# Raw float64 weight blocks converted in pairs: one VectorE shift, one mask and one ScalarE reading over 1024 elements instead of two over 512

## The chip, the cores and the metric

One core of a Trainium2 chip runs the whole program: TensorE (PE, matmuls; its weight loads are PEld), VectorE (DVE), ScalarE (ACT), GpSimd (POOL) and SyncE (SP), which issues most of the DMAs. The metric is the device time of one launch in microseconds. The kernel before took 1313.93 to 1318.08 us in three runs, median 1317.09 us.

## What is computed

```python
# 1 attention, 4 batches x 8 heads x 576 tokens x 64, of each row the 32 largest scores
scores = scale * q @ k.T; keep = scores >= kth_largest(scores, 32)
x = softmax(where(keep, scores, -1e9)) @ v          # -> 2304 tokens x 512
# 2 gated layer; w_a, w_b [512, 1536] and w_out [1536, 512] arrive as float64
x = ((x @ w_a) * (x @ w_b)) @ w_out
# 3 one of 8 experts per token, chosen by cosine with expert_emb; gate = its softmax weight
out[t] = gate[t] * (relu(x[t] @ w1[e]) @ w2[e])
```

[...] A block of 128x512 weights is loaded as raw 64-bit words and its bits are put together to float32 by integer work; the float32 number is then split into two float32r parts (high and low), and each product of the gated layer is the sum of three matmuls over these parts.

## The kernel before, in words

**Attention runs in steps.** One step treats one tile of 128 attention rows; there are 144. For a tile TensorE makes scores, ScalarE copies them to `s`, VectorE takes the 32 largest (`topk`, lines 369 to 391: four MAX8 and three MATCH_REPLACE8 over 576 elements), ScalarE and GpSimd make the softmax weights (`softmax`, lines 393 to 403), TensorE turns and multiplies them. In step n VectorE does the first half of tile n and the second half of tile n-1, woven together.

**The weights are converted beside the first 30 steps or so.** `Blocks` (line 492) holds 36 blocks in a fixed order: (0,f) and (1,f) are column blocks of w_a and w_b, (2,f) row blocks of w_out. A block goes through: loading of the raw words by SP (line 515, 512 KB); a ScalarE reading of the low words (line 535); on VectorE a shift with a mask of the high words (line 538) and a second mask (line 539); a GpSimd addition that gives float32 in `x1T` (line 543); a ScalarE rounding to the high part (line 551); two TensorE passes (lines 554 and 555) and a ScalarE copy for the low part (line 556); for w_a and w_b a store to DRAM (line 558), from which later token groups read them again. The code has one state per block (`at`): `open` issues line 535, `start` lines 538, 539 and the next load, and each call of `stage` moves a block on by one: to 2 (addition), 3 (line 551), 4 (lines 554 to 558).

**Buffers.** Two raw blocks (`raw64`, RB = 2), two of each half-product (`w64t`, `w64r`, TB = 2), two of `x1T` (XB = 2), four of `wab` (WB = 4). A raw buffer is free when lines 535, 538 and 539 of its block have read it; only then SP can issue the load that takes its place. `may` also holds a w_a or w_b block back until the gated layer of the first token group has come to hidden block f-1 (`begun`).

**Order.** TensorE, VectorE, ScalarE and GpSimd execute in the order in which the Python code emits; SP's queue is ordered by a planner with priorities. In a step the code emits VectorE's `topk`, then five slots of TensorE work with `background` work of the gated layer between them; `conv.stage()` is called in slots 0, 2 and 4, `conv.open()` in slot 3, and `conv.start()` at the step's end. From step 16 on two blocks are started per step, before that one in every second step. A second use of `raw64`: token groups with odd number take two of these buffers for their input (line 618), and so does the first expert (line 1157).

After attention the remaining token groups and then the experts run, almost on TensorE alone.

Of the kernel before, what the change touches and what calls it, by code (L numbers as in the profile page):

```python
# [26 lines left out]
GN = 256  # L27
# [16 lines left out]
RB = 2  # L44
FOLD = (0,)
PEN = (0,)
PC = 512
TB = 2
UEV = 2.6
EARLY = 6  # L50
# [24 lines left out]
FG = 100000  # L75
# [7 lines left out]
def fused_kernel(  # L83
# [18 lines left out]
    pe, dve, act, pool, sp = nc.tensor, nc.vector, nc.scalar, nc.gpsimd, nc.sync  # L102
# [93 lines left out]
    mk = mo.enter_context(tc.tile_pool(name="mk", bufs=2))  # L196
    mp = mo.enter_context(tc.tile_pool(name="mp", bufs=2, space=PSUM))

    with ExitStack() as ph:
        wk = ph.enter_context(tc.tile_pool(name="wk", bufs=2, side="right"))  # L200
# [291 lines left out]
        class Blocks:  # L492
# [3 lines left out]
            def __init__(self):  # L496
                self.order = [(i, f) for f in range(2) for i in range(2)] + [(2, f) for f in range(EARLY)]
                for f in range(2, NF):
                    self.order += [(0, f), (1, f)] + [(2, f + EARLY - 2)] * (f + EARLY - 2 < NF)
                self.raw, self.tiles, self.begun, self.at, self.going = [], {}, 0, [], []  # L500

            def fetch(self, n):
                while len(self.raw) < min(n, len(self.order)):
                    i, f = self.order[len(self.raw)]
                    if i < 2:
                        src = (w_a, w_b)[i][:, f * P : (f + 1) * P].rearrange("(c p) j -> p c j", p=P)
                    else:
                        src = w_out[f * P : (f + 1) * P, :].rearrange("p (c j) -> p c j", c=KC)
                    if src.dtype == F32:
                        raw = mk.tile([P, KC, P], F32, name="raw64", bufs=RB)  # L510
                        sp.dma_start(raw, src)
                    else:
                        raw = mk.tile([P, KC, P, 2], I32, name="raw64", bufs=RB)
                        with tc.high_priority(offset=2 * FG if len(self.raw) < EL else FG):
                            sp.dma_start(raw.rearrange("p a n t -> p a (n t)"), src.bitcast(I32))
                    self.raw.append(raw)

            def may(self, k):

# [6 lines left out]

            def block(self, k):
                i, f = self.order[k]
                raw = self.raw[k]
                if raw.dtype == F32:  # L530
                    x = raw
                else:
                    lo, hi = raw[:, :, :, 0], raw[:, :, :, 1]
                    r = wk.tile([P, KC, P, 2], I16, name="w64r", bufs=TB)
                    act.activation(r[:, :, :, 0], lo.bitcast(U32), AF.Copy, scale=2.0**-29)
                    yield
                    t = wk.tile([P, KC, P], I32, name="w64t", bufs=TB)
                    dve.tensor_scalar(t, hi, 3, 0x3FFFFFFF, op0=OP.logical_shift_left, op1=OP.bitwise_and)
                    dve.tensor_scalar(r[:, :, :, 1], raw.bitcast(I16)[:, :, :, 3], -0x4000, None, op0=OP.bitwise_and)
                    self.fetch(k + 1 + RB)  # L540
                    yield
                    x = mk.tile([P, KC, P], F32, name="x1T", bufs=XB)
                    pool.tensor_tensor(x.bitcast(I32), t, r.rearrange("p a n t -> p a (n t)").bitcast(I32), op=OP.add)
# [12 lines left out]
                act.activation(lo, p.rearrange("p (c j) -> p c j", c=KC), AF.Copy)  # L556
                if i < 2:
                    sp.dma_start(wab_d[i, f], wt.bitcast(F32).rearrange("p a c j -> p (a c j)"))

# [3 lines left out]
                    self.stage()  # L563

            def ready(self, *block):
                return block in self.order[: sum(a == 4 for a in self.at)]

            def open(self):

                k = len(self.at)  # L570
                if k < len(self.order) and sum(a < 2 for a in self.at) < TB:
                    self.fetch(k + RB)
                    self.going.append(self.block(k))
                    self.at.append(0)
                    if self.raw[k].dtype != F32:
                        next(self.going[k])
# [10 lines left out]
            def stage(self):  # L587

                for k in range(len(self.at)):
                    if 0 < self.at[k] < 4 and self.may(k):  # L590
                        next(self.going[k], None)
                        self.at[k] += 1

        conv = Blocks()
# [6 lines left out]
        class Group:  # L601
# [5 lines left out]
            def inputs(self):  # L607
                if self.xg:
                    return
                g0, N = GROUPS[self.gi]  # L610
                self.xg = []
                if self.gi == 0 and DIRECT:
                    self.xg = xg0
                    return
                conv.need(1, NF - 1)
                for i, d in enumerate((xh_d, xl_d)):
# [295 lines left out]
        for step in range(-AHEAD_L, NRW + TL + 5):  # L912
            now[0] = step
            if step + AHEAD_L < NRW:
                b, pr, part, first, last, kind, c, slot = rows[step + AHEAD_L]
# [6 lines left out]
            if 0 <= step + AHEAD_P < NRW:  # L922
                b, pr, part, first, last, kind, c, slot = rows[step + AHEAD_P]
# [9 lines left out]
            j = step - 2  # L933
# [3 lines left out]
            with tc.high_priority(offset=FG):  # L937
                next(soft, None)
                soft = softmax(live[step - 2]) if 0 <= step - 2 < NRW else none
                j = step - 5  # L940
                if 0 <= j < NRW and rows[j][4] and made[rows[j][:3]].n >= F0 * NP:
                    sums(made[rows[j][:3]], False)
                j = step - 3
# [12 lines left out]
                elif 0 <= step < NRW:  # L956
                    thresholds[0] = cur
            if step == -AHEAD_L:
                conv.fetch(RB)
# [16 lines left out]
            if i != turned[0] + 1:  # L976
                i = -1
# [15 lines left out]
            for slot_, g in enumerate((tg, sg, tg, mg, sg)):  # L993
                if g is not none and not run(g) and g is mg and mixes:
                    mixes.pop(0)
                    mg = none
                with tc.high_priority(offset=FG):
                    if slot_ == 1 or slot_ == (2 if mg is not none else 3):
                        next(soft, None)
                    if slot_ in (0, 2, 4) and step >= 2:  # L1000
                        conv.stage()
                    if slot_ == 3:
                        for _ in range(pace):
                            conv.open()
                if slot_ in (2, 4):
                    piece()
# [21 lines left out]
            for _ in range(pace):  # L1028
                with tc.high_priority(offset=FG):
                    conv.start()  # L1030
            while done < len(GROUPS) and (sum(GROUPS[done]) <= ready[0] or (done == 0 and ready[0])):
                w = step + (D0 if done == 0 else RD)
                todo.append([w, Group(done, w), None])
                if done and len(todo) < 3 and conv.ready(1, NF - 1):
                    todo[-1][1].inputs()
                    if len(todo) == 1:
                        todo[-1][1].load()
                done += 1
        order.__exit__(None, None, None)

    with ExitStack() as ph:
# [111 lines left out]
        def first_expert():  # L1153

            ids = wx.tile([P, 2, 2], I32, name="ids0")
            sp.dma_start(ids, idv[0, : 2 * P, :].rearrange("(t p) c -> p t c", p=P))
            xs = [mk.tile([P, PC // KC * KC * 2], F32, name="raw64", bufs=RB)[:, :RW] for _ in range(2)]
# [103 lines left out]
        for e in range(1, NE):  # L1261
            nx = gather(e + 1) if e + 1 < NE else None
            xs, xT = x
# [97 lines left out]
```

## Time and profile before

| | us |
|---|---|
| median of three runs | 1317.09 |
| profiled execution | 1316.72 |
| its span, first to last instruction | 1315.0 |
| PE busy | 1173.2 |
| DVE busy | 921.4 |
| ACT busy | 820.2 |
| POOL busy | 720.9 |
| mean granted TensorE clock | 0.965 of full |

The busy times are averages over stages with different limits, so the table alone does not say what sets the end. The profile splits the span into windows and shows there which engine has no idle time left; it also shows, per instruction, what ended the idle time before it.

### The profile page before, as it was taken

Reading aid. Unit: us, or ns where it says so; the run is one execution under the profiler, and the core shown is the slowest. Engines: PE = TensorE matmul, PEld = TensorE weight load, DVE = VectorE, ACT = ScalarE, POOL = GpSimd, SP = SyncE. Lnnn points to the kernel's source line nnn. Section 1 sums busy time; section 2 is a strip of 40 time slices with the busy share of each in tenths; the row PEclk is TensorE's granted clock in tenths of the full one; section 3 lists DMA queues with packets and bytes.
Section 4 is the critical chain, followed back from the end, with each engine's and each line's share of the span. In section 5 each row is a group of like instructions: output and inputs, shape, how many; then the busy total and the mean of one; then the engine's idle time right before and its main releaser. Section 6 shows DMA issues by size and latency. Waiting matters only on the chain. (4 is left out here: it accounts for less than half of the span.)

```text
span 1315.0 us, 23367 instructions
## 1 busy us (share of the span) xinstructions
PE 1173.2 (89%) x7908; PEld 988.1 (75%) x7909; DVE 921.4 (70%) x1995; ACT 820.2 (62%) x1964; POOL 720.9 (55%) x1188
## 2 busy tenths in 40 slices
PE   5667978879999987999998998899999989999996
PEld 3445656767898766888886886777898868888885
DVE  8998998989889888999988899750200145444440
ACT  5876978777777776777777776663432344444441
POOL 5665786667667775677677766564545321111100
PEclk8888999999999997999999999899999989999999
DMA  7424775557685654766665667458987046555520
GB/s 234 148 95 143 243 233 169 188 172 215 202 260 173 180 157 161 199 194 202 193 199 164 208 182 211 136 157 282 326 291 248 18 131 212 174 170 168 173 87 20
DMA packets 129102, 240.57 MB, mean 183 GB/s; under 512 B 24621, under 2 KB 73901, under 8 KB 128978
## 3 DMA queue, kind: packets, MB, share of 16 engines
q1 hardware_dynamic: 124818, 228.74, 55.2%
q0 software_dynamic: 4160, 10.29, 2.4%
q8 instruction: 64, 1.05, 0.3%
q14 instruction: 60, 0.49, 0.1%
HBM read 198.92 MB, written 40.85 MB: 182 GB/s over the span
## 5 line engine op out<-in xcount | busy, mean ns | idle before, releaser
L386 DVE MAX8 t<-y 128x8 f32<-128x576 f32 x432 | 312.2, 750 | 3.0
L401 POOL TENSOR_TENSOR z<-s,z 128x576 f32<-128x576 f32 x144 | 206.0, 1431 | 105.1 <-ACT z L398 99.1
L389 DVE MATCH_REPLACE8 y<-t,y 128x576 f32<-128x576 f32 x288 | 214.0, 743 | 0.0
L721 PE MATMUL ab<-xg,wab 128*128 128x256 f32 x1398 | 207.9, 291 | 5.8 <-ACT gab L735 3.1
L721 PEld LDWEIGHTS ab<-xg,wab 128*128 128x128 f32 x1398 | 184.0, 192 | 9.6 <-ACT gab L735 3.5
L721 PE MATMUL ab<-raw,wab 128*128 128x256 f32 x1152 | 172.7, 290 | 7.2 <-ACT gab L735 5.0
L420 PE MATMUL tr<-ident,z 128*128 128x128 f32 x720 | 134.1, 286 | 37.0 <-ACT z L403 29.1
L721 PEld LDWEIGHTS ab<-raw,wab 128*128 128x128 f32 x1152 | 151.0, 192 | 11.2 <-ACT gab L735 5.9
L403 ACT ACTIVATE z<-z,bi 128x576 f32<-128x576 f32 x144 | 111.7, 775 | 69.9 <-POOL z L401 69.9
L365 PE MATMUL tr<-kT,qT 128*128 128x288 f32 x512 | 127.5, 332 | 25.8 <-ACT qT L342 13.8
L386 DVE MAX8 t<-s 128x8 f32<-128x576 f32 x144 | 107.7, 748 | 49.7 <-ACT s L366 42.1
L366 ACT ACTIVATE s<-tr 128x288 f32<-128x288 f32 x288 | 118.8, 413 | 35.6 <-PE tr L365 34.3
L423 ACT ACTIVATE wt<-tr 128x384 f32<-128x384 f32 (+2 forms) x320 | 127.7, 414 | 17.5 <-PE tr L420 16.8
L668 PE MATMUL x<-wo,gh 128*128 128x512 f32 x432 | 135.4, 395 | 0.0
L1067 DVE TENSOR_TENSOR u<-raw,u 128x1024 fp32r<-128x1024 f32 x64 | 76.2, 1221 | 83.7 <-ACT u L1066 61.8
L1116 POOL DMA_INDIRECT out_dram<-o,ids x24 | 24.0, 999 | 200.9 <-ACT o L1115 197.6
L655 POOL TENSOR_TENSOR gab<-gab 128x256 f32<-128x256 f32 x108 | 82.5, 764 | 91.5 <-ACT gab L735 81.7
L420 PEld LDWEIGHTS tr<-ident,z 128*128 128x128 f32 x720 | 90.3, 145 | 53.7 <-ACT z L403 35.5
L1144 PE MATMUL y<-u,hT 128*128 128x512 f32 (+1 forms) x528 | 128.0, 396 | 0.4 <-DVE hT L1249 0.4
L365 PEld LDWEIGHTS tr<-kT,qT 128*128 128x128 f32 x512 | 87.0, 203 | 38.4 <-ACT qT L342 16.2
L398 ACT ACTIVATE z<-s,bi 128x576 f32<-128x576 f32 x144 | 112.8, 784 | 0.5 <-DVE bi L391 0.5
L1144 PEld LDWEIGHTS y<-u,hT 128*128 128x128 f32 (+1 forms) x528 | 89.7, 173 | 27.6 <-DVE hT L1249 0.5
(187 smaller groups left out, 2231.5 us busy)
## 6 DMA issues: line engine op xcount, KB each, us to landing
wab<-wab_d SPq DMA_DIRECT2D x192, 512.0 KB, 4.4
raw<-in_moe_w_dram SPq DMA_DIRECT2D x28, 1024.0 KB, 6.1
wab_d<-wab SPq DMA_DIRECT2D x24, 512.0 KB, 4.0
kT<-kT_d SPq DMA_DIRECT2D x20, 576.0 KB, 5.5
vs<-in_v_dram SPq DMA_DIRECT2D x36, 256.0 KB, 3.6
kT_d<-kT SPq DMA_DIRECT2D x16, 576.0 KB, 5.0
raw<-in_moe_w_a_dram SPq DMA_DIRECT2D x12, 512.0 KB, 4.1
raw<-in_moe_w_b_dram SPq DMA_DIRECT2D x12, 512.0 KB, 5.2
```

The source lines that it names most:

```text
L365: pe.matmul(p, l, r, start=(i == 0), stop=(i == len(terms) - 1))
L366: act.activation(t.s[:, cs], p, AF.Copy, scale=SCALE)
L386: dve.max(v, cur)
L389: dve.match_replace(out=rest, in_to_replace=v, in_values=cur, imm_value=LOWEST)
L398: act.activation(t.w, t.s, AF.Relu, bias=t.bi[:, 1:2], scale=-HUGE)
L401: pool.tensor_tensor(t.w, t.s, t.w, op=OP.subtract)
L403: act.activation(t.w, t.w, AF.Exp, bias=t.bi[:, 0:1], accum_out=t.o.sm[:, t.slot : t.slot + 1])
L420: pe.transpose(pt[:, i * P : (i + 1) * P], t.w[:, k0 : k0 + P], ident)
L423: act.activation(th[:, sl, w], pv[:, :, src], AF.Copy)
L668: pe.matmul(px[t], g[:, ts], wo[:, w, f], start=(f == 0 and i == 0), stop=(f == NF - 1 and i == 2))
L721: pe.matmul(ps_[i], wt[:, a, c, :], xg[x][:, c, :], start=(j == 0 and f not in begun), stop=(j == len(terms) - 1),)
L1144: pe.matmul(p[:m], (hi, lo)[a], u[:, b, f % 4, :], start=(f == 0 and i == 0), stop=(f == NF2 - 1 and i == 2))
```

## The change

Two neighbouring blocks of the order become a pair. The order is rearranged so that a pair is always of one kind: for an even f two w_out blocks follow (0,f), (1,f), for an odd f none. A pair has one raw tile with two halves, loaded by two DMAs; there is one such tile where there were two single ones, and one `w64t` and one `w64r` of double length. The first block of a pair issues one ScalarE reading, one shift and one mask over 1024 elements, and with them the loads of the next pair; the second block issues none of these. The addition, rounding, TensorE passes and copy stay per block. The addition comes by a `stage` call at the step's end, behind `start`; the other `stage` calls move from slots 0, 2 and 4 to slots 1 and 3; the store to DRAM becomes a state of its own (5), one `stage` call after line 556. The first block starts at step 0 and not at step -1, and steps 0 to 3 start one block each. The two inputs of an odd token group, and the first expert's two tiles, are halves of one raw tile.

```diff
-                    self.order += [(0, f), (1, f)] + [(2, f + EARLY - 2)] * (f + EARLY - 2 < NF)
+                    self.order += [(0, f), (1, f)] + [(2, f + EARLY - 2 + j) for j in range(2) if f % 2 == 0] * (
+                        f + EARLY - 2 < NF
+                    )
...
+                    for j in range(2):
...
+                        if pair is None:
+                            pair = mk.tile([P, 2, KC, P * (2 if wide else 1)], I32 if wide else F32, name="raw64", bufs=1)
                         with tc.high_priority(offset=2 * FG if len(self.raw) < EL else FG):
-                            sp.dma_start(raw.rearrange("p a n t -> p a (n t)"), src.bitcast(I32))
-                    self.raw.append(raw)
+                            sp.dma_start(pair[:, j], src.bitcast(I32) if wide else src)
+                        self.raw.append(pair)
...
+                    if j == 0:
+                        w = raw.rearrange("p a c (n t) -> p (a c n) t", t=2)
+                        r = wk.tile([P, 2 * KC * P, 2], I16, name="w64r", bufs=1)
+                        act.activation(r[:, :, 0], w[:, :, 0].bitcast(U32), AF.Copy, scale=2.0**-29)
+                        yield
+                        t = wk.tile([P, 2 * KC * P], I32, name="w64t", bufs=1)
+                        dve.tensor_scalar(
+                            t, w[:, :, 1], 3, 0x3FFFFFFF, op0=OP.logical_shift_left, op1=OP.bitwise_and
+                        )
+                        dve.tensor_scalar(r[:, :, 1], w.bitcast(I16)[:, :, 3], -0x4000, None, op0=OP.bitwise_and)
+                        self.pair = t, r
+                        self.fetch(k + 4)
+                    else:
+                        yield
                     yield
...
                 act.activation(lo, p.rearrange("p (c j) -> p c j", c=KC), AF.Copy)
+                yield
                 if i < 2:
                     sp.dma_start(wab_d[i, f], wt.bitcast(F32).rearrange("p a c j -> p (a c j)"))
...
-                if k < len(self.order) and sum(a < 2 for a in self.at) < TB:
-                    self.fetch(k + RB)
+                if k < len(self.order) and (k % 2 or all(a > 1 for a in self.at)):
+                    if k % 2 == 0 and len(self.raw) <= k:
+                        if any(a < 4 for a in self.at):
+                            return
+                        self.fetch(k + 2)
...
+                if self.gi % 2:
+                    both = mk.tile([P, 2, KC, GN], F32R, name="raw64", bufs=1)
...
-                        t = mk.tile([P, KC, GN], F32R, name="raw64", bufs=RB)
+                        t = both[:, i]
...
-            pace = int(step >= -1) if step < 2 else (step + 1) % 2 if step < 16 else 2
+            pace = int(step >= 0) if step < 4 else (step + 1) % 2 if step < 16 else 2
...
-                    if slot_ in (0, 2, 4) and step >= 2:
+                    if slot_ in (1, 3):
                         conv.stage()
...
             for _ in range(pace):
                 with tc.high_priority(offset=FG):
                     conv.start()
+            with tc.high_priority(offset=FG):
+                conv.stage()
```

## Rows read from the trace of the kernel before

**Rows 1.** Windows by stage: length, busy us (instructions) per engine, clock, DMA, GB/s
```profile
0.00:103.00 103.00, 62.55 (x345) 43.50 (x346) 97.79 (x227) 74.33 (x171) 57.65 (x85) 0.86 0.46 152
103.00:224.00 121.00, 100.06 (x582) 74.78 (x583) 109.93 (x212) 94.91 (x209) 86.22 (x96) 0.94 0.64 211
...
275.00:875.00 600.00, 551.22 (x4167) 471.73 (x4166) 532.42 (x1220) 434.08 (x1145) 410.25 (x724) 0.97 0.63 190
```
**Rows 2.** Windows, the same columns, of seven steps with two blocks each
```profile
131.50:188.90 57.40, 51.18 (x283) 36.27 (x282) 56.72 (x108) 52.83 (x116) 48.11 (x51) 1.00 0.71 227
```
**Rows 3.** Instructions by line, whole span: min/median/max ns, first to last start us
```profile
L538 DVE TENSOR_SCALAR w64t<-raw x36: 398/428/1665, 8.6 to 223.4; 128x512 int32<-128x512 int32 x36
...
L539 DVE TENSOR_SCALAR w64r<-raw x36: 439/466/1710, 9.0 to 223.7; 128x512 int16<-128x512 int16 x36
```
**Rows 4.** Groups by line, window 103 to 224: busy us, mean ns, idle before, releaser
```profile
L538 DVE TENSOR_SCALAR w64t<-raw 128x512 int32<-128x512 int32 x27 | 20.3, 751 | 11.0 <-POOL x1T L543 9.3 <-DMA raw<-in_moe_w_b_dram 1.4 <-DMA raw<-in_moe_w_out_dram 0.3
...
L539 DVE TENSOR_SCALAR w64r<-raw 128x512 int16<-128x512 int16 x27 | 24.3, 900 | 0.0
...
L391 DVE TENSOR_SCALAR bi<-t 128x1 f32<-128x1 f32 x14 | 1.9, 133 | 0.0
...
L543 POOL TENSOR_TENSOR x1T<-w64t,w64r 128x512 int32<-128x512 int32 x25 | 32.4, 1308 | 8.6 <-PE tr L554 2.5 <-DVE t L386 2.4 <-ACT kT L326 1.2
```
**Rows 5.** Window 0 to 103, line 538 alone: length, VectorE busy (instructions), clock, DMA, GB/s
```profile
0.00:103.00 103.00, 5.36 (x9) 0.86 0.46 152
```
**Rows 6.** VectorE, order of time: start us, us, engine, line, operation
```profile
13.54 0.42 DVE L538 TENSOR_SCALAR w64t<-raw 128x512 int32<-128x512 int32 x1
13.88 0.46 DVE L539 TENSOR_SCALAR w64r<-raw 128x512 int16<-128x512 int16 x1
14.22 0.75 DVE L386 MAX8 t<-y 128x8 f32<-128x576 f32 x1
...
131.50 0.75 DVE L386 MAX8 t<-y 128x8 f32<-128x576 f32 x1
...
136.46 0.42 DVE L538 TENSOR_SCALAR w64t<-raw 128x512 int32<-128x512 int32 x1
136.79 1.53 DVE L539 TENSOR_SCALAR w64r<-raw 128x512 int16<-128x512 int16 x1
138.22 0.42 DVE L538 TENSOR_SCALAR w64t<-raw 128x512 int32<-128x512 int32 x1
138.56 1.66 DVE L539 TENSOR_SCALAR w64r<-raw 128x512 int16<-128x512 int16 x1
```
**Rows 7.** GpSimd in the same steps, order of time
```profile
135.10 2.90 POOL L543 TENSOR_TENSOR x1T<-w64t,w64r 128x512 int32<-128x512 int32 x2 [2.22 <-DVE t L386]
...
138.32 1.58 POOL L401 TENSOR_TENSOR z<-s,z 128x576 f32<-128x576 f32 x1
```
**Rows 8.** Waits of VectorE, then of ScalarE, 100 to 226: us, times, longest
```profile
DVE w64t L538 <- POOL x1T L543: 9.3, 2, 6.0
...
ACT w64r L535 <- DMA raw<-in_moe_w_b_dram: 5.3, 2, 3.7
```
**Rows 9.** SP in order of time, two loads issued one behind the other
```profile
132.25 0.38 SPq L515 DMA_DIRECT2D raw<-in_moe_w_a_dram  x1
132.89 0.38 SPq L515 DMA_DIRECT2D raw<-in_moe_w_b_dram  x1
...
205.30 0.38 SPq L515 DMA_DIRECT2D raw<-in_moe_w_a_dram  x1
205.93 1.25 SPq L515 DMA_DIRECT2D raw<-in_moe_w_b_dram  x1
```
**Rows 10.** Time to landing: of the loads at 132.89 and 205.93, of all
```profile
DMA to landing us min/median/max: 5.2/5.2/5.2
...
DMA to landing us min/median/max: 6.4/6.4/6.4
...
DMA to landing us min/median/max: 3.2/4.2/6.4
```
**Rows 11.** Groups, whole span: matmuls of the odd token groups, their releasers
```profile
L721 PE MATMUL ab<-raw,wab 128*128 128x256 f32 x1152 | 172.7, 290 | 7.2 <-ACT gab L735 5.0 <-DMA wab<-wab_d 2.2
```

More of the change, by code (lines that the diff above doesn't have):

```diff
@@ L503, in fetch @@
                 while len(self.raw) < min(n, len(self.order)):
[L504 to L513, printed above, removed]
+                    pair = None
+                    for j in range(2):
+                        i, f = self.order[len(self.raw)]
+                        if i < 2:
+                            src = (w_a, w_b)[i][:, f * P : (f + 1) * P].rearrange("(c p) j -> p c j", p=P)
+                        else:
+                            src = w_out[f * P : (f + 1) * P, :].rearrange("p (c j) -> p c j", c=KC)
+                        wide = src.dtype != F32
+                        if pair is None:
+                            pair = mk.tile([P, 2, KC, P * (2 if wide else 1)], I32 if wide else F32, name="raw64", bufs=1)
                         with tc.high_priority(offset=2 * FG if len(self.raw) < EL else FG):
-                            sp.dma_start(raw.rearrange("p a n t -> p a (n t)"), src.bitcast(I32))
-                    self.raw.append(raw)
+                            sp.dma_start(pair[:, j], src.bitcast(I32) if wide else src)
+                        self.raw.append(pair)
             def may(self, k):
@@ L528, in block @@
                 i, f = self.order[k]
-                raw = self.raw[k]
+                raw, j = self.raw[k], k % 2
                 if raw.dtype == F32:
-                    x = raw
+                    x = raw[:, j]
                 else:
-                    lo, hi = raw[:, :, :, 0], raw[:, :, :, 1]
-                    r = wk.tile([P, KC, P, 2], I16, name="w64r", bufs=TB)
-                    act.activation(r[:, :, :, 0], lo.bitcast(U32), AF.Copy, scale=2.0**-29)
-                    yield
[L537 to L541, printed above, removed]
-                    x = mk.tile([P, KC, P], F32, name="x1T", bufs=XB)
-                    pool.tensor_tensor(x.bitcast(I32), t, r.rearrange("p a n t -> p a (n t)").bitcast(I32), op=OP.add)
+                    if j == 0:
[10 more added lines that the diff above has]
+                        self.fetch(k + 4)
+                    else:
+                        yield
+                    yield
+                    t, r = self.pair
+                    h = slice(j * KC * P, (j + 1) * KC * P)
+                    x = mk.tile([P, KC, P], F32, name="x1T", bufs=XB)
+                    pool.tensor_tensor(
+                        x.rearrange("p c j -> p (c j)").bitcast(I32),
+                        t[:, h],
+                        r[:, h].rearrange("p n t -> p (n t)").bitcast(I32),
+                        op=OP.add,
+                    )
@@ L565, in ready @@
             def ready(self, *block):
-                return block in self.order[: sum(a == 4 for a in self.at)]
+                return block in self.order[: sum(a >= 4 for a in self.at)]
             def open(self):
                 k = len(self.at)
-                if k < len(self.order) and sum(a < 2 for a in self.at) < TB:
-                    self.fetch(k + RB)
+                if k < len(self.order) and (k % 2 or all(a > 1 for a in self.at)):
[3 more added lines that the diff above has]
+                        self.fetch(k + 2)
                     self.going.append(self.block(k))
@@ L589, in stage @@
                 for k in range(len(self.at)):
-                    if 0 < self.at[k] < 4 and self.may(k):
+                    if 0 < self.at[k] < 5 and self.may(k):
                         next(self.going[k], None)
@@ L615, in inputs @@
                 conv.need(1, NF - 1)
+                while any(a < 5 for a in conv.at):
+                    conv.stage()
+                if self.gi % 2:
+                    both = mk.tile([P, 2, KC, GN], F32R, name="raw64", bufs=1)
                 for i, d in enumerate((xh_d, xl_d)):
                     if self.gi % 2:
-                        t = mk.tile([P, KC, GN], F32R, name="raw64", bufs=RB)
+                        t = both[:, i]
                     else:
@@ L958, in fused_kernel @@
             if step == -AHEAD_L:
-                conv.fetch(RB)
-            pace = int(step >= -1) if step < 2 else (step + 1) % 2 if step < 16 else 2
+                conv.fetch(2)
+            pace = int(step >= 0) if step < 4 else (step + 1) % 2 if step < 16 else 2
             if step == 4:
@@ L1030, in fused_kernel @@
                     conv.start()
+            with tc.high_priority(offset=FG):
+                conv.stage()
             while done < len(GROUPS) and (sum(GROUPS[done]) <= ready[0] or (done == 0 and ready[0])):
@@ L1156, in first_expert @@
             sp.dma_start(ids, idv[0, : 2 * P, :].rearrange("(t p) c -> p t c", p=P))
-            xs = [mk.tile([P, PC // KC * KC * 2], F32, name="raw64", bufs=RB)[:, :RW] for _ in range(2)]
+            both = mk.tile([P, 2, PC // KC * KC * 2], F32, name="raw64", bufs=1)
+            xs = [both[:, i, :RW] for i in range(2)]
             for t in range(2):
```

## The prediction

> **What bounds the kernel now.** I read the windows by stage first, because the share of busy time over the whole span mixes an attention stage with an expert stage. Up to 103 us VectorE is the engine without idle time: 97.79 of 103 us busy, TensorE 62.55 [rows 1]. From 103 to 224 us, where two blocks are converted per step, nobody is alone at the limit: VectorE 109.93, TensorE 100.06, ScalarE 94.91 of 121. In seven of these steps VectorE is busy 56.72 of 57.40 us and ScalarE 52.83, so that a step takes 8.2 us and ScalarE has 0.65 us of it to spare [rows 2]. From 275 us on TensorE is at 551.22 of 600 [rows 1]. The chain of waits, looked at next, is of no use here: it follows the last scatter and no further. So a microsecond taken from the first 224 us comes off the end, because the work behind it keeps its order and waits for nothing with a time of its own; the change touches no instruction behind 275 us but the two buffers of the odd token groups.
>
> The groups by line show what the conversion costs VectorE. A shift has a median of 428 ns, a mask of 466 [rows 3]; between 103 and 224 us their means are 751 and 900 over 27 blocks [rows 4]. The reason stands in the order of time. At 13.54 us a shift, mask and the next MAX8 follow each other by 0.34 us. At 136.79 the mask takes 1.53 us and at 138.56 it takes 1.66 [rows 6]: it ends when GpSimd's addition (135.10, 2.90 us for two) or its subtraction (138.32, 1.58 us) ends [rows 7]. A shift or mask thus stands behind the GpSimd instruction that is under way; MAX8 beside the same engine keeps its 0.75.
>
> **The change, part by part.** Working against the profiled execution, 1316.7 us, which is 0.4 below the median of the runs.
>
> *Half as many instructions.* 72 shifts and masks become 36 of double length. No row has one of 1024 elements. The least a join can save is nothing; the most is the whole of a nearly empty instruction, 133 ns for 128x1 [rows 4], 36 times: 4.8 us. Instructions overlap, though: 0.42 long, 0.34 apart [rows 6], so 0.08 to 0.09 of the 0.133 is hidden already. I take 0.045 x 36 = 1.6 us: 0.4 in the first 103 us, 1.2 after.
> The Trainium skill, "VectorE: DVE Perf Modes", section "The TRN2 errata — SBUF-src ops pay a fixed extra latency per instruction", gives 58 cycles beside half a cycle per element at 0.96 GHz for such an operation, 327 ns for 512, which the spacing of 0.34 bears out. By it a join saves 0.06 us, and the term would be 2.2 us.
>
> *The standing behind GpSimd.* Over the medians, 103 to 224 us: 27 x (0.751 - 0.428) = 8.7 and 27 x (0.900 - 0.466) = 11.7, together 20.4 us. Before 103 us: nine shifts 5.36 [rows 5] less 9 x 0.428, 1.5; masks taken alike, so 3.0. What an instruction waits for is the rest of one GpSimd instruction, whatever its own length, so half as many wait half as long: 10.2 and 1.5 saved. Ends: nothing, if each long one meets a GpSimd instruction and now waits for what two waited for, and all 23.4, if GpSimd already stands at the addition. That can be, as the addition comes about one slot earlier; in the trace it waited 2.4 us for VectorE there [rows 4]. I take the half.
>
> *One raw tile for two.* Before, the load into a buffer started after its own block's mask, while VectorE still did the other block. Now both loads start after the pair's mask, and the next shift needs both. Between two conversions VectorE has 131.50 to 136.46 = 4.96 us of its own [rows 6]. Two loads issued together needed 0.64 + 5.2 = 5.8 us at 132.25 and 0.63 + 6.4 = 7.05 us at 205.30 to the second landing [rows 9, 10]; a single one has a median of 4.2. So VectorE, and ScalarE whose reading sits in its queue before the evictions of the scores, waits 0, 0.85 or 2.1 us per pair. I take 0.85, the row nearest to a pair with little beside it, because the stores come a `stage` call later and so behind the loads. Thirteen pairs in successive steps: 11.0 us; ScalarE's 5.3 us for single loads [rows 8] are in this and go: net +5.7. Ends: -5.3 and +22. In steps 4 to 15 a pair comes every fourth step, and its load has time.
>
> *One ScalarE reading for two.* Two readings take about what one double one does less a start; 0 to 0.1 us per pair, in an engine with 0.65 to spare per step: 0.
>
> *The later start.* The first block's shift and mask lay at 8.6 us [rows 3], before the first scores; they now come at step 0's end with the second block's, in VectorE's full time: +0.7.
>
> *Addition and stores.* Two additions (1.31 each [rows 4]) stand in GpSimd's queue before the next step's subtraction as they did in slot 0; at most one slot earlier. If GpSimd waits there for the mask, the subtraction, ScalarE's exponential and the turning behind it come later by that much; the turning is three or four steps behind `topk`, so 0. A store that comes one call later holds its `wab` tile; the first reload is after the last block: 0. Where stores stood in SP's queue ahead of loads, these now go first.
>
> *Odd token groups.* Their two inputs share one tile. The 1152 matmuls that read it waited 7.2 us in all, none of it for that input [rows 11]: 0.
>
> Sum: first 103 us -0.4 - 1.5 + 0.7 = -1.2; then -1.2 - 10.2 + 5.7 = -5.7; together -6.9: 1309.8 us, and with the 0.4 of the median 1310. Per dense step this takes 0.44 of 8.2 us, which ScalarE's 0.65 allows.
>
> **Rivals.**
>
> *Slower: the single tile is the new bound.* If the pair's loads land as at 205.30 each time, VectorE and ScalarE wait 2.1 us in 13 steps: 27 - 5.3 = +22, against -10.2 - 1.2 - 1.2: +9, 1326 us. It decides from a wait of 1.4 us per pair, a landing 6.3 us after the first issue. For it: DMA was busy 0.71 in these steps [rows 2], and of the two pairs that can be read one is above that. Against it: the row at 132.25 was in the same steps.
> The Trainium skill, "Trainium Kernel Development and Optimization", section "Best Practices", says to double-buffer so that loading and computing overlap, which this change gives up; by that rule this rival would be the outcome, 1326. The trace agrees in so far as single loads with two buffers still made ScalarE wait 5.3 us.
>
> *No difference: TensorE's order sets the stretch.* The last blocks are held until the gated layer has come far enough, and the two long stalls of VectorE, 9.3 us [rows 8], came from additions behind TensorE's passes (L554 in [rows 4]). TensorE had 100.06 of 121 us to do [rows 1]. What VectorE gains it would then lose in longer stalls; the early 1.2 us and perhaps two more stay: 1314 to 1316.
>
> *Much faster.* GpSimd stands ready at the addition, nothing is in VectorE's way, and -23.4 - 1.6 + 0.7 + 5.7 = -18.6. ScalarE's floor allows 0.65 x 13 = 8.5 in the dense steps, with the early 3 about 11.5, and more if a stall goes: 1302.
>
> *It doesn't do what it says.* If an instruction over 1024 elements ran at half the rate per element, (0.428 - 0.133) x 2 = 0.59 us more each, 36 times 21 us: against the gains of 6.9, 1331.
>
> **How the numbers follow.** Forecast 0.38 (its own range 1305 to 1313), no difference 0.28, slower by the tile 0.18, much faster 0.12, half rate 0.04. A measurement can tell about 0.3%, 4 us, from no change. Faster: the forecast and the much faster case, 0.50. Same: 0.28. Slower: 0.22. The range leaves out the far end of the slow cases and of the fast one: 1300 to 1324.
>
> **What would show it.** After: 18 shifts and 18 masks with medians near 0.70 and 0.74 us, and means not over 1.1 in the dense steps (half the standing). ScalarE's and VectorE's waits for the raw loads near 0.85 us per pair, some 11 us in all; far more means the slow rival, near nothing means that I overpaid. The last mask at about 217 us where it was 223.7. If it comes earlier but the end does not, the work behind has taken the gain; if the stalls on the additions grow past 9.3 us, TensorE's order decides. Wrong altogether if the medians of the long instructions are over 1.2 us.

## The result, and the profile after

The changed kernel takes 1324.9 us (median of nine runs, 1322.62 to 1329.5), the kernel before in the same comparison 1317.89 (nine runs, 1313.93 to 1322.55): ratio 1.0059, 95% interval 1.0042 to 1.0077. It is slower by 0.6%, some 7.8 us, where 0.5% less was forecast. The profiled execution of after, 1329.5 us with a span of 1327.7, is the longest of its nine; that of before, 1316.72, is below its median. Of the 12.7 us between the two spans not all is the change, therefore, and what I take from the two traces below was tested by runs.

The windows by stage come first, as in [rows 1], with the same columns:

```profile
0.00:103.00 103.00, 65.46 (x329) 45.73 (x331) 95.68 (x219) 72.15 (x158) 57.49 (x82) 0.82 0.48 157
103.00:224.00 121.00, 98.96 (x583) 73.53 (x583) 92.22 (x183) 94.46 (x196) 83.25 (x99) 0.94 0.59 203
```

VectorE's busy time fell as the change wants it: 109.93 to 92.22 us in the second stage. But the stage isn't shorter; the 17.7 us became idle time. As a marker of a step I take the start of the first MAX8 that reads `s` in it (counted from step 0): step 31, about where the conversions end, starts at 224.76 us before and at 227.00 after.

The instructions by line (least/median/longest in ns, first to last start), for [rows 3]:

```profile
L541 DVE TENSOR_SCALAR w64t<-raw x18: 676/782/1922, 13.4 to 223.8; 128x1024 int32<-128x1024 int32 x18
...
L544 DVE TENSOR_SCALAR w64r<-raw x18: 741/758/1992, 14.2 to 225.7; 128x1024 int16<-128x1024 int16 x18
...
L538 ACT ACTIVATE w64r<-raw x18: 1353/1366/1412, 14.4 to 223.8; 128x1024 int16<-128x1024 uint32 x18
```

The long instructions do full work per element, 0.78 and 0.76 us for twice 0.43 and 0.47. The groups by line between 103 and 224 us, for [rows 4] (busy us, mean ns, idle before, releasers):

```profile
L553 POOL TENSOR_TENSOR x1T<-w64t,w64r 128x512 int32<-128x512 int32 x24 | 30.3, 1284 | 10.1 <-ACT w64r L538 6.6 <-ACT gh L678 2.6 <-ACT wab L571 0.8
...
L541 DVE TENSOR_SCALAR w64t<-raw 128x1024 int32<-128x1024 int32 x13 | 14.3, 1104 | 28.7 <-DMA raw<-in_moe_w_b_dram 11.2 <-POOL x1T L553 10.8 <-DMA raw<-in_moe_w_out_dram 6.3
L544 DVE TENSOR_SCALAR w64r<-raw 128x1024 int16<-128x1024 int16 x12 | 11.1, 921 | 0.0
```

Ahead of the shift VectorE was idle 28.7 us where it was 11.0. Raw loads made it wait 11.2 and 6.3, together 17.5 us, against 1.7 before in this window [rows 4] and 2.0 up to 250 us. ScalarE and GpSimd waited too (total, times, longest, first 250 us):

```profile
ACT w64r L538 <- DMA raw<-in_moe_w_b_dram: 3.7, 3, 1.7
```
```profile
POOL x1T L553 <- ACT w64r L538: 10.3, 5, 2.7
```

The second line is new. GpSimd's addition now comes so early that ScalarE's reading isn't done; before, no addition waited for the reading. Why the loads are late, the order of time shows. VectorE, ScalarE and SP around one pair (start, length, then idle time before and its releaser in brackets):

```profile
149.58 0.77 DVE L544 TENSOR_SCALAR w64r<-raw 128x1024 int16<-128x1024 int16 x1
...
160.06 0.69 DVE L541 TENSOR_SCALAR w64t<-raw 128x1024 int32<-128x1024 int32 x1 [4.79 <-DMA raw<-in_moe_w_b_dram]
```
```profile
150.78 1.39 ACT L538 ACTIVATE w64r<-raw 128x1024 int16<-128x1024 uint32 x1
...
160.14 1.37 ACT L538 ACTIVATE w64r<-raw 128x1024 int16<-128x1024 uint32 x1 [1.70 <-DMA raw<-in_moe_w_b_dram]
161.37 0.39 ACT L366 ACTIVATE s<-tr 128x288 f32<-128x288 f32 x1
```
```profile
150.40 0.32 SPq L574 DMA_DIRECT2D wab_d<-wab  x1
150.81 0.38 SPq L302 DMA_DIRECT2D kT<-kT_d  x1
151.25 0.78 SPq L574 DMA_DIRECT2D wab_d<-wab  x1
152.20 0.38 SPq L517 DMA_DIRECT2D raw<-in_moe_w_a_dram  x1
152.63 1.55 SPq L517 DMA_DIRECT2D raw<-in_moe_w_b_dram  x1
```

The mask of the pair ends at 150.35. The next loads go out at 152.20 only, and two things hold them. ScalarE's reading of the same raw tile, which stands behind the copies and roundings of its queue, ran from 150.78 to 152.17. But SP's queue also has two stores and a load of keys ahead of them, and was free at 152.03 only. The second load has landed by 160.06, 7.9 us after the first issue. ScalarE itself then waits 1.70 us, and the copy of the scores (L366) stands behind its reading. The reading isn't always last: of the twelve pairs loaded from 109.50 us on, it ended over 0.5 us later than the mask in six, by 0.7 to 4.4 us. The three longest waits for loads, 12.7 of the 17.5 us, follow the three pairs where it was 4.4, 1.8 and 3.2 us later. In the first of these nothing stood ahead of the loads in SP's queue; in the other two a store held it to 152.03 and 178.70, so that the reading alone held the loads for 0.1 and 0.9 us.

The second place lies behind the conversions. From step 31 to step 39 after is 2.2 us late; step 43 starts 7.5 us late (298.09 against 290.64). Here the first token group of the gated layer ends and its routing begins. GpSimd before, then after, in order of time:

```profile
266.59 0.67 POOL L219 TENSOR_SCALAR ks<-kr 128x576 fp32r<-128x576 f32 x1
...
267.41 1.43 POOL L401 TENSOR_TENSOR z<-s,z 128x576 f32<-128x576 f32 x1
...
269.29 0.58 POOL L767 TENSOR_TENSOR st<-st,half 128x1 f32<-128x1 f32 x1
...
270.83 0.55 POOL L767 TENSOR_TENSOR st<-st,half 128x1 f32<-128x1 f32 x1
...
271.88 1.40 POOL L221 TENSOR_TENSOR ks<-kr,ks 128x576 fp32r<-128x576 f32 x1
```
```profile
272.98 0.58 POOL L790 TENSOR_TENSOR st<-st,half 128x1 f32<-128x1 f32 x1 [3.24 <-ACT x1T L789]
...
274.08 0.68 POOL L219 TENSOR_SCALAR ks<-kr 128x576 fp32r<-128x576 f32 x1
...
274.92 1.42 POOL L401 TENSOR_TENSOR z<-s,z 128x576 f32<-128x576 f32 x1
...
276.76 0.57 POOL L790 TENSOR_TENSOR st<-st,half 128x1 f32<-128x1 f32 x1
...
277.83 1.40 POOL L221 TENSOR_TENSOR ks<-kr,ks 128x576 fp32r<-128x576 f32 x1
```

Line 790 of after is line 767 of before (the routing of a token tile), L219 and L221 split the next batch's keys, L401 is the softmax subtraction. Before, the first half of the split and the subtraction stand ahead of both routings; GpSimd waits for nothing. After, the first routing has moved ahead of both: GpSimd waits 3.24 us for ScalarE's square of a result that TensorE has yet to finish, and keys and subtraction wait behind it. TensorE in the same place, before and after:

```profile
273.34 0.88 PE L308 MATMUL tr<-identr,ks 128*128 128x128 f32 x8 [3.51 <-POOL ks L221]
...
275.09 4.05 PE L461 MATMUL tr<-wt,vs 128*64 128x256 f32 x20
...
280.51 0.95 PE L778 MATMUL ab<-enT,x1T 128*128 128x8 f32 x8
```
```profile
279.29 1.26 PE L308 MATMUL tr<-identr,ks 128*128 128x128 f32 x8 [5.37 <-POOL ks L221]
...
281.76 1.20 PE L744 MATMUL ab<-raw,wab 128*128 128x256 f32 x4
282.76 1.71 PE L801 MATMUL ab<-enT,x1T 128*128 128x8 f32 x8
284.40 4.12 PE L461 MATMUL tr<-wt,vs 128*64 128x256 f32 x20
```

TensorE stands 5.37 us instead of 3.51 on the keys, and the choice of the expert (L801, L778 before) now runs ahead of the attention mix (L461) instead of behind it: from the turning of the keys to the end of the mix it takes 9.2 us (279.29 to 288.52) against 5.8. Behind the mix the copy of the next scores is late, and VectorE stands 5.27 us at 290. Eight steps later, ahead of step 50, it stands again, behind GpSimd:

```profile
290.13 0.76 DVE L386 MAX8 t<-s 128x8 f32<-128x576 f32 x1 [5.27 <-ACT s L366]
```
```profile
DVE t L386 <- POOL xsb L473: 3.1, 1, 3.1
```

### The profile page after: what moved, and what is told of

Read it like the earlier page. It is cut to its first block, busy times and chain, and to the rows that moved or that the text cites. A ratio compares the mean times of both kernels' runs of the same rounds, so it can differ in the third digit from the quotient of the medians.

```text
span 1327.7 us, 23275 instructions
## 1 busy us (share of the span) xinstructions
PE 1184.3 (89%) x7908; PEld 1000.0 (75%) x7909; DVE 904.3 (68%) x1959; ACT 821.3 (62%) x1946; POOL 720.1 (54%) x1188
## 5 line engine op out<-in xcount | busy, mean ns | idle before, releaser
L401 POOL TENSOR_TENSOR z<-s,z 128x576 f32<-128x576 f32 x144 | 205.9, 1430 | 109.7 <-ACT z L398 103.7
L744 PE MATMUL ab<-raw,wab 128*128 128x256 f32 x1152 | 176.7, 296 | 8.6 <-ACT gab L758 4.8
L744 PEld LDWEIGHTS ab<-raw,wab 128*128 128x128 f32 x1152 | 154.9, 197 | 12.8 <-ACT gab L758 6.1
L365 PE MATMUL tr<-kT,qT 128*128 128x288 f32 x512 | 129.9, 337 | 25.8 <-ACT s L366 13.0
L366 ACT ACTIVATE s<-tr 128x288 f32<-128x288 f32 x288 | 118.7, 412 | 32.1 <-PE tr L365 30.7
L691 PE MATMUL x<-wo,gh 128*128 128x512 f32 x432 | 138.1, 401 | 0.0
L365 PEld LDWEIGHTS tr<-kT,qT 128*128 128x128 f32 x512 | 90.3, 207 | 41.6 <-ACT s L366 15.8
```

The lines of the kernel that those rows point to most:

```text
L365: pe.matmul(p, l, r, start=(i == 0), stop=(i == len(terms) - 1))
L366: act.activation(t.s[:, cs], p, AF.Copy, scale=SCALE)
L401: pool.tensor_tensor(t.w, t.s, t.w, op=OP.subtract)
L691: pe.matmul(px[t], g[:, ts], wo[:, w, f], start=(f == 0 and i == 0), stop=(f == NF - 1 and i == 2))
L744: pe.matmul(ps_[i], wt[:, a, c, :], xg[x][:, c, :], start=(j == 0 and f not in begun), stop=(j == len(terms) - 1),)
```

## The experiments

Theory A: two costs, the raw load held by ScalarE's reading in the conversions, and the order at the hand-over to routing, which the moved `stage` calls turn. A block becomes `ready` earlier, the first token group's work is emitted some four matmuls earlier, and GpSimd's routing slips ahead of the keys. Rivals are named with each run. Measured are the ratio to before, from the same chip, with its 95% interval (before itself had a median of 1320.94 us beside e1 to e4, 1320.23 beside e5 to e8 and 1320.87 beside e9 to e11, so that the ratios compare across the table and the times don't); "keys" is TensorE's wait on `ks` in the trace, "40 to 43" the time between those two steps.

| run | us | ratio (interval) | step 31 | keys | 40 to 43 |
|---|---|---|---|---|---|
| before, profiled | 1317.89 | 1 | 224.76 | 3.5 | 20.1 |
| before, second profile (e12) | | | 222.94 | 3.5 | 19.5 |
| after | 1324.90 | 1.0059 (1.0042 to 1.0077) | 227.00 | 5.4 | 24.9 |
| e1 | 1323.18 | 1.0024 (1.0006 to 1.0041) | 227.77 | 3.5 | 20.2 |
| e2 | 1325.43 | 1.0043 (1.0027 to 1.0058) | 225.24 | 5.4 | 21.3 |
| e3 | 1330.20 | 1.0067 (1.0042 to 1.0093) | 225.77 | 5.4 | 24.2 |
| e4 | 1329.45 | 1.0063 (1.0042 to 1.0084) | 227.11 | 5.4 | 22.9 |
| e5 | 1323.89 | 1.0038 (1.0022 to 1.0054) | 223.98 | 5.4 | 20.9 |
| e6 | 1325.45 | 1.0032 (1.0012 to 1.0051) | 229.08 | 3.5 | 20.7 |
| e7 | 1324.08 | 1.0027 (1.0009 to 1.0044) | 225.06 | 5.4 | 25.2 |
| e8 | 1322.27 | 1.0016 (1.0000 to 1.0032) | 227.09 | 3.4 | 20.7 |
| e9 | 1320.40 | 0.9998 (0.9983 to 1.0013) | 223.20 | 3.5 | 21.7 |
| e10 | 1330.87 | 1.0083 (1.0054 to 1.0112) | 233.00 | 3.5 | 20.1 |
| e11 | 1325.10 | 1.0037 (1.0021 to 1.0053) | 224.80 | none | 21.4 |

**How far two traces differ (e12).** The kernel before, unchanged, profiled once more.

> The kernel before, profiled a second time, for how far two traces of one kernel differ: the steps to 39 within 1 us, the part behind step 138 within 4 us (478.3 in the first), the stalls of the shifts and masks behind GpSimd within 5 us of 23.4.

Step 39 came 1.8 us earlier than in the first trace, more than I had expected, step 96 5.4 us earlier, and from step 138 on it took 481.9 us where the first took 478.3. So a single trace can't settle 2 us at step 31 or 5 us at step 96, and the 3.4 us by which after is longer behind step 138 (481.7) need no cause in the change. What does repeat is the wait on the keys: 3.5 us in both, and 3.4 to 3.5 in every trace with that order.

The second wait repeats as well. The six traces with the turned order (after, e2, e3, e4, e5, e7) have VectorE standing 3.0 to 3.3 us behind GpSimd ahead of step 50, and from step 49 to 50 they take 8.2 to 8.5 us. The six others with the order of before take 5.2 to 5.3 (e11 apart, which has an order of its own), and e8 takes 6.4. Part of it is given back at once: steps 43 to 54 take 61.7 to 61.9 us with the turned order and 59.7 to 59.8 with the other (e8 60.9). From step 39 to 54 the turned order takes 88.0 to 92.6 us, the other 84.3 to 86.6, e8 among them.

**The hand-over: after with the order put back (e1), before with it turned (e2).** What a piece of background work yields is its price against the budget of a slot; a higher price once puts what follows into a later slot. Changed is one such value of the first token group, at one place, so that the emission order changes from there on:

```diff
-                    yield 0.64
+                    yield 0.64 + (0.4 if gi == 0 and f == NF - 3 and t == 0 else 0.0)   # e1; e2: -0.4
```

> The changed kernel with one cost of the background work raised once, by 0.4 us of budget near the end of the first token group; this alone puts GpSimd's routing of the first token tile behind the rounding of the next keys again, as in the kernel before. Theory A (about 5 us of the loss arise after the conversion, where this order is turned): 1320 us, ratio to before 1.002, and VectorE's distance to the kernel before stays near +2 us from step 31 through step 60. Rival B (the loads of the pairs cost it all): no change, 1325 us, ratio 1.006.

> The kernel before with that cost lowered once by 0.4, which gives it the changed kernel's order at the hand-over and nothing else. Theory A: 5 us slower than before, 1323 us, ratio 1.004. Rival B: as before, 1318 us, ratio 1.000.

Both came as theory A has it. e1 takes 0.35 of the 0.59% away (the two intervals just miss each other), e2 adds 0.43% to a kernel that is otherwise the one before. e1 stays 3.0 to 3.1 us behind the first trace of before from step 31 to step 54; e2 is 1.6 us behind it at step 43 and 3.9 at step 54, so that the wait on the keys alone isn't the whole cost. GpSimd in e1 has the keys ahead again, and TensorE's waits in e2 show the longer stall:

```profile
268.79 0.67 POOL L219 TENSOR_SCALAR ks<-kr 128x576 fp32r<-128x576 f32 x1
...
269.62 1.45 POOL L401 TENSOR_TENSOR z<-s,z 128x576 f32<-128x576 f32 x1
...
271.51 0.58 POOL L790 TENSOR_TENSOR st<-st,half 128x1 f32<-128x1 f32 x1
```
```profile
PE tr L308 <- POOL ks L221: 5.4, 1, 5.4
```

**Which edit turns it: the stage move alone (e5), the pairs alone (e6).**

```diff
 # e5: the kernel before, blocks singly
-                    if slot_ in (0, 2, 4) and step >= 2:
+                    if slot_ in (1, 3):
                         conv.stage()
...
+            with tc.high_priority(offset=FG):
+                conv.stage()
```

e6 is the changed kernel with these two places put back.

> The kernel before (blocks singly, two raw tiles) with only the additions moved: stage calls in slots 1 and 3 and one at the step's end. Theory A (the moved stage calls alone let the first token group's work run ahead, so that at 270 to 290 us GpSimd takes the group's routing ahead of the next keys): the marker of VectorE's steps jumps by 3 to 5 us between steps 40 and 43, and the ratio to before is about 1.003 to 1.005. Rival B (it is the pairing that does it): no jump there, ratio 1.000 within 0.001. On the stalls behind GpSimd: if they fell from 23.4 to 7.5 us because the additions come earlier, the single shifts and masks (26 each) fall below 35 us of busy time before 224 us here, as against 41.8 before; if they fell because the instructions are half as many, they stay at 40 or more.

> The changed kernel with the addition's stage calls put back in slots 0, 2 and 4 from step 2 on, and no stage at the step's end: the pairs alone. Theory A: no jump at steps 40 to 43, and what is left is the pairs' own cost, some +2 to +3 us at step 31 that stays, ratio 1.002 (1.001 to 1.0035). Rival B (the pairs turn the hand-over): the jump of 4 to 7 us is there, ratio 1.005 to 1.006. Stalls of the shifts and masks over 0.69 and 0.76 us: near 7.5 us as in the changed kernel if halving the instructions did it, 12 or more if the earlier addition did it.

The stall on the keys settles it: 5.4 us in e5, 3.5 in e6. The moved calls turn the order; pairs do not. Both ratios lie where theory A had them. The marker of e5 doesn't: 0.8 us more than before between steps 40 and 43, not 3 to 5. The mix ran at another speed there: its 20 matmuls took 2.53 us in e5 and 4.12 in after, so the later place cost less in that execution. In e6 the 4.3 us at step 31 and the 0.32% are the pairs' own cost.

**The stage move alone with the order put back (e8).** e5 with the pace value of e1.

> The stage move alone on the kernel before (as in the first of these), with 0.4 of a matmul unit added once to the first group's pace so that GpSimd's order at the hand-over is that of the kernel before. Theory A: no jump at steps 40 to 43, ratio 1.000 within 0.0015; if the additions at the step's end also shorten the stalls behind GpSimd, the conversions end 1 to 3 us earlier and the ratio is 0.998. Rival B (the hand-over has nothing to do with GpSimd's order): the same ratio as the stage move alone.

1.0016, between the two: the stall is back at 3.4 us, but the interval overlaps that of e5. The conversions did not end earlier.

**A second raw tile (e3).** It lies in the space of the last two row blocks of `wo`, so that pair is converted last; e4 is the control with that order alone.

```diff
-   pair = mk.tile([...], name="raw64", bufs=1)
+   pair = mk.tile([...], name=("raw64", "wot")[len(self.raw) // 2 % 2], bufs=1)
...
-                        self.fetch(k + 4)
+                        self.fetch(k + 6)
```

> The changed kernel with a second raw tile for pairs (it lies where the last two row blocks of w_out go, whose pair is converted last). Loads are then issued a whole pair ahead. Theory A and B both: VectorE's waits for raw loads fall from 17.5 us to under 3 us; A with the hand-over still turned: the stretch is 10 to 12 us shorter, 1314 us, ratio 0.997. Rival C (ScalarE and TensorE set the stretch, the load wait only fills their slack): under 4 us gained, 1321 to 1325 us.

> The changed kernel with only the order of e3 (the last w_out pair at the end), one raw tile. All theories: as the changed kernel, 1325 us, ratio 1.006, waits for raw loads 15 to 20 us.

Of theory A only the first half came: the waits for raw loads fell from 16.3 (e4) to 2.9 us. The time fits rival C: nothing was gained. VectorE's waits in e3:

```profile
DVE w64t L557 <- POOL x1T L569: 25.8, 9, 9.3
DVE w64t L557 <- DMA raw<-in_moe_w_b_dram: 2.9, 1, 2.9
```

The next single buffer took over. `w64t` is free when GpSimd has added both halves, and that wait went from 14.0 (e4) to 25.8 us. Step 31 came 1.3 us earlier than in e4, less than two traces of one kernel differ, and the time is that of the control.

**ScalarE's reading away from the raw tile (e7), and with the order put back as well (e9).** The reading has the same shape and engine but takes a resident tile; the low 32 bits of the weights are left out.

```diff
-  act.activation(r[:, :, 0], w[:, :, 0].bitcast(U32), AF.Copy, scale=2.0**-29)
+  act.activation(r[:, :, 0].rearrange("p (a n) -> p a n", a=8),
+                 ident.bitcast(U32).unsqueeze(1).to_broadcast([P, 8, P]), AF.Copy, scale=2.0**-29)
```

> The changed kernel with ScalarE's reading of 1024 low halves taken from a resident tile instead of the raw pair (same shape and engine; the low 32 bits of each weight are left out). A load then waits for the mask alone. Theory A (the load of the next pair is held by ScalarE's late reading, and TensorE and ScalarE set the stretch): VectorE's waits for raw loads before 250 us fall from 17.5 to 6 to 11 us, its waits for w64t from GpSimd rise, step 31 comes within 1 us of where it came, and the time stays within 0.2% of the changed kernel (ratio to before 1.004 to 1.008). Rival B (the raw loads are what the stretch waits for): step 31 comes 4 to 8 us earlier and the ratio to before is 1.002 or less.

> The changed kernel with both suspected costs taken away: ScalarE's reading from a resident tile (the low 32 bits of each weight are left out) and GpSimd's order at the hand-over put back by 0.4 of a matmul unit. Theory A (two costs, the raw load held by ScalarE's late reading, some 2 to 4 us, and the hand-over, some 3 to 5 us, make up the loss): step 31 within 1 us of before, no jump at steps 40 to 43, ratio 1.000 (0.998 to 1.0015). Rival B (the pairs cost something else as well, or the two don't add): ratio 1.002 or more.

VectorE's waits in e7:

```profile
DVE w64t L541 <- POOL x1T L553: 18.5, 6, 9.3
DVE w64t L541 <- DMA raw<-in_moe_w_b_dram: 4.0, 4, 1.3
...
DVE w64t L541 <- DMA raw<-in_moe_w_out_dram: 1.2, 1, 1.2
```

The load waits fell to 5.2 us, the waits on the additions rose by 7.7, and step 31 came 1.9 us earlier than after: between what A and B expected, and so is the time, 0.32% below after. I had taken the reading for worth less. e9, with both costs gone, is level with before at 0.9998: the two add up, and of the 0.59% nothing is left over that 0.15%, its interval, could show. Its step 31 came 1.6 us earlier than in the first trace of before, and steps 40 to 43 took 1.6 us longer; both are within what the two traces of before differ by. What these two runs can't part is how the reading costs. It holds the next load; it makes ScalarE's own queue wait for the load (3.7 us after, three times); and it holds GpSimd's addition (10.3 us in after, 6.8 in e7, 4.7 in e9). A fourth thing changed with it: in e7 the planner put the loads ahead of the two stores that stood before them in after. SP in e7, at the same pair:

```profile
152.24 0.38 SPq L517 DMA_DIRECT2D raw<-in_moe_w_a_dram  x1
...
153.22 0.51 SPq L574 DMA_DIRECT2D wab_d<-wab  x1
```

No run moved the stores alone. And e3 took the waits for loads away without gaining anything, so what e7 gives back is not VectorE's wait for loads by itself. In e6 the addition hardly waits for the reading (0.2 us) and the pairs cost 0.32% all the same, so that the hold on the addition isn't needed for the cost either. What is left stays open.

**Starting early again (e10).** e1 with blocks started from step -1 as before.

> The changed kernel with GpSimd's order at the hand-over put back and blocks started from step -1 on as in the kernel before. Theory A (TensorE and ScalarE set the stretch, and the later start is worth little): ratio within 0.001 of the 1.0024 that the order alone gave. Rival B (the pairs' 3 us at step 31 are the later start): step 31 within 1 us of before and ratio 1.000 or less.

Neither: 1.0083. VectorE in e10:

```profile
13.84 0.69 DVE L541 TENSOR_SCALAR w64t<-raw 128x1024 int32<-128x1024 int32 x1 [5.63 <-DMA vs<-in_v_dram]
...
15.09 0.74 DVE L386 MAX8 t<-s 128x8 f32<-128x576 f32 x1
```

The first MAX8 starts at 15.09 instead of 10.19: the shift stands ahead of it and needs the pair's second load, issued at 8.73 behind the loads of queries and values (the trace names a load of values that landed about then). With pairs the later start isn't a cost of 0.7 us, as I had it, but a repair. e10 is 8.25 us later than before at step 31: 3.0 of it are in e1 already, and the first MAX8 is 4.6 us later than in e1 (15.09 against 10.51); the rest is within what two traces differ by.

**The order turned the other way (e11).** Before with a pace value of +0.8 at the same place, which sets the key split between the two routings.

> The kernel before with 0.8 of a matmul unit added once to the first group's pace at the hand-over, which puts GpSimd's second half of the key split ahead of the second token tile's routing. Theory A (each split of keys that stands behind a routing costs at the hand-over): the stall of 3.5 us of TensorE on the keys near 285 us goes, steps 43 to 48 come 1 to 4 us earlier, ratio 0.997 to 0.999. Rival B (only the first split matters, or the time is given back by step 60): ratio 1.000 within 0.001.

A miss: TensorE no longer waits on the keys (1.9 us remain there, for a copy of scores), yet the ratio is 1.0037. GpSimd now waits 2.2 us ahead of the first routing and VectorE 2.5 us for the threshold (`bi`) that stands behind it in GpSimd's queue; by step 54 the trace is 6.7 us behind the first of before. The order of the kernel before is better than its neighbours on either side; most of this one's loss lies in VectorE's waits ahead of step 50 (3.7 us, for scores) and in step 51 (3.8, for the routing); why they grow stays open. No run was faster than before, so there is no better version to show.

## Why the prediction was wrong, by its steps

*Work behind keeps its order, additions and stores cost 0: this step failed.* I costed the moved `stage` calls at GpSimd's queue within a step and asked only who waits for the addition there. The calls also set when a block counts as `ready`, hence where the first token group's matmuls stand in the emission, and at that group's end where its routing stands in GpSimd's queue, 50 us behind the last conversion. Priced by e1 it is 0.35% (4.6 us), by e2 0.43% (5.7 us). Two more steps of that term did not hold. The addition was to wait for VectorE's mask at most; it waited 10.3 us for ScalarE's reading, and it did so for 4.7 to 10.3 us in all nine traces with the moved calls (e5, with single blocks, 7.5), against at most 0.2 in the five without them (e6, the pairs alone, 0.2). And loads were to go ahead of stores in SP's queue; at 152.20 two stores went first. What these two cost by themselves no run shows.

*One raw tile for two: mechanism right, size wrong.* I took 0.85 us a pair, 11.0 us, from two rows in which the load went out after the mask. VectorE's waits for loads were 17.5 us and ScalarE's 3.7: the load waits for the last of three readers, which in six of twelve pairs is ScalarE's, and for the stores ahead of it. [rows 2] had the sign of it: with 0.65 us to spare per step ScalarE has no reason to be early. By e7 against after the reading with all that hangs on it is worth 0.32%, by e9 against e1 0.26%, 3.4 us; the intervals overlap in each of the two comparisons, but both have the same sign and size.
The Trainium skill, "Trainium Kernel Development and Optimization", section "Best Practices", has double-buffering as a rule; the run that did it for the load alone (e3) gained nothing, and its wait for the next single buffer rose from 14.0 to 25.8 us.

*Standing behind GpSimd: better than forecast.* Over [rows 3]'s medians the 72 shifts and masks of before stood 23.4 us. After, the 36 have 34.0 us (18.4 and 15.6), over 0.69 and 0.76 each 7.9 us. The fall of 15.5 compares with 11.7 forecast; against the second trace of before, which has 19, it is 11. It comes from the number of instructions, not from the earlier addition: e6, the pairs alone, has 9.9 us, e5, the stage move alone, about 17. The prediction reads the end of a long mask as the end of GpSimd's instruction; by its rows the mask ends 0.32 us behind it, both times (138.32 against 138.00, 140.22 against 139.90).
The Trainium skill, "SBUF — State Buffer", section "Who interferes with whom", says that in VectorE's two-port modes, which `tensor_scalar` can enter, the engine that issues first blocks the other for its whole instruction. That fits a price per instruction, as I had assumed; no run here shows the mode.

*The join: right.* From shift to MAX8 two single blocks take 2 x 0.68 us [rows 6]; after, 148.97 to 150.25, 1.28. That is 0.08 a pair, 1.4 us in all against 1.6.

*A microsecond from the first 224 us comes off the end: wrong.* VectorE gained 17.7 us in busy time in the second stage and lost 15.5 in waits for loads and 1.5 in waits for additions. With both costs gone (e9) the kernel is level with before and no faster, so the shorter standing bought nothing there either. Each single tile (raw, then `w64t`) hands the time on, as the waits of e3 and e7 show; that a chain of single buffers through ScalarE and GpSimd set the pace, though VectorE was the busiest engine, fits these waits but was not tested by itself. The sign that the prediction gave for TensorE's order came, stalls on the additions of 10.8 us where they were 9.3, but without its cause: the additions waited for ScalarE. The slower rival had the right side and nearly the time (1326 against 1324.9), with half of the cause: it knew nothing of the hand-over, so that its number is luck in part.

## What to carry to other kernels

When a tile has several readers, its reload waits for the last of them, and for what stands ahead of it in the queue that issues it; look up both before pricing the load. Before halving the buffers for longer instructions, follow the chain to the next single buffer. When engines run in emission order, a moved call can reorder work far behind the stage it belongs to: compare the order of each queue at the next hand-over, and price that too.

## What the hardware showed that I had not expected

The granted TensorE clock makes the same reordering cost different amounts. TensorE in windows of 5 us at the hand-over of after, and of e2 (length, busy us, clock, DMA, GB/s):

```profile
275.00:280.00 5.00, 0.71 (x6) 0.74 0.00 0
280.00:285.00 5.00, 5.00 (x28) 0.50 0.24 69
285.00:290.00 5.00, 5.00 (x37) 0.73 0.02 5
```
```profile
270.00:275.00 5.00, 0.37 (x3) 0.75 0.20 68
275.00:280.00 5.00, 4.26 (x27) 0.56 0.23 62
280.00:285.00 5.00, 5.00 (x47) 1.00 0.19 54
```

In both TensorE was nearly idle in the first window. Behind it after had the lower level, 1.2 of 2.4 GHz, through the next window and into the third; e2 was back at the full clock in the third. The 20 matmuls of the mix took 4.12 us in after, 3.91 in e3 and 4.43 in e7, but 2.53 in e2, e4 and e5 with the same order of routing and keys. With the slow mix steps 40 to 43 took 24.2 to 25.2 us, with the fast one 20.9 to 22.9. The slow mix isn't a mark of the turned order: before had it too, 4.05 us. So medians of many runs, not one trace, priced the order.
